# Held-back loads, block products for two more slabs, ScalarE copies and a new order at the end of a Fourier mixer with a gated FFN

## The chip, the core and the metric

The kernel runs on one core of a Trainium2 chip. A core has TensorE (matrix products, into PSUM banks), VectorE (DVE in the profile), ScalarE (ACT), GpSimd (POOL) and SyncE (SP, which issues most DMA transfers). Each engine works through its own instructions in order; semaphores tie the engines together. The metric is device microseconds of one execution, as the median of several runs; a profiled execution gives the trace.

## The reference, cut to what matters

```python
x = A_x                                   # 1 x 2048 x 640, bf16
xn = _layernorm(x, axis=-1)
s = irfft2(rfft2(xn, axes=(-2, -1)) * (w_r + 1j * w_i), s=(2048, 640))
g = silu((gelu(xn @ w_gate) * (xn @ w_up)) @ w_down)      # F = 1536
return x + s * g
```

So every row is normalized; the normalized matrix goes through a two-dimensional Fourier filter (s) and through a gated FFN (g), and the two meet in the last line. Layernorm is over the 640 columns, gelu is the tanh form, and everything is bf16 outside of the transform.

## The kernel before, in words

The 2048 rows are taken as 16 slabs of 128 rows (slab n1 holds the rows n1, n1+16, ...), `X[:, n1, :]`. Four slabs make a group g of 512 rows. For each group the FFN goes over 12 tiles of 128 hidden columns: a gate product (`psg`, five matmuls, then gelu by ScalarE into `ge`, L837), an up product (`psu`, five matmuls, L832), and on VectorE `psu * ge` into `UT` (L839). Then the down product: for groups 0 and 3 slab by slab (`down_third`, L967, 24 matmuls of 320 columns for a slab), for groups 1 and 2 as block products of two slabs (`product`, L933): seven products of six matmuls in place of 48 matmuls for a pair of slabs, over sums of blocks of `UT` that VectorE makes (`u_sum`, L907) and sums of blocks of Wd (`w_sum`). Results of products are copied out by ScalarE (L937) and added on VectorE (L947). Then silu (`gated`, L861 to L882) gives G.

`psg` and `psu` have two PSUM banks each, and so has the pool `psB`, which the transposes and all stages of the Fourier filter share.

The order of the work is written by hand. `back` is a list of 144 steps, most of them an FFN half tile (1.08 us of TensorE) or a product; `plan[s]` lists what is put behind step s, and `put` fills it. Instructions are issued in just that order, so it is also the order in every engine's queue. The Fourier filter is spread over the steps: forward stages (`slab_S1`, `slab_D`) during groups 0 and 1, a middle stage in eleven bursts (`s2_step`, from step `sb` = 67 on; its input comes through DRAM, ZDR to `B2`, and its result leaves through DRAM, UDR to V), inverse stages (`slab_S1i` L735, `slab_Di` L762, and the VectorE and ScalarE work of `group_cs`, `group_Y`, `group_rest` for three slabs at a time) during the products of group 2 and all of group 3. `finish(n1)` multiplies s by G (L811), adds x (for slabs 12 to 15 on VectorE, L815; for the others by an accumulating DMA) and writes out. It runs whenever a half of a slab is ready.

At the start SP loads x0, x1, then weights of Wu in twos of tiles between further slabs, and ScalarE's queue loads Wg (L231). The DMA semaphores are used in turn, eight of them, so the ninth transfer waits for the first one's landing, and so on. Statistics of a slab are two `bn_stats` halves and an aggregate on VectorE; the root of the variance comes from ScalarE for slab 0 (`root_act`) and from GpSimd for the others (`root`). `norm_parts` normalizes a slab in two parts, columns 0 to 384 and 384 to 640; `slab_Tparts` transposes those parts on TensorE and copies them to `xnT`. TensorE first runs 21 matmuls on constants (`warm_pe`, L588).

Of the kernel before, what the change touches and what calls it, by code (L numbers as in the profile page):

```python
# [10 lines left out]
BF16 = mybir.dt.bfloat16  # L11
# [3 lines left out]
P = 128  # L15
# [61 lines left out]
def build(nc, env):  # L77
# [19 lines left out]
    load_w(1, 2, 4)  # L97
    load_x(2, 1)
    load_w(1, 4, 6)
    load_x(3, 1)  # L100
    load_gu(6, 8)
    load_x(4, 4)
    load_gu(8, 12)
    load_x(8, 4)
    nc.sync.dma_start(out=Wd, in_=B_w_down.rearrange("(t p) d -> p t d", p=P))
    load_x(12, 4)

# [104 lines left out]
    def root_act(n1):  # L212
        rstd[n1] = c1("rst0")
        nc.scalar.activation(out=rstd[n1], in_=mva[n1 // 4][:, n1 % 4, 1:2], func=ACT.Abs_reciprocal_sqrt, bias=eps)
        nc.scalar.activation(out=warm, in_=negpi, func=ACT.Gelu_apprx_tanh)

# [110 lines left out]
    vt_iota(0)  # L327
    stats(0)
    bn_half(1, 0)
# [474 lines left out]
    def finish(n1):  # L804
        ks = [k for k in range(len(cut(n1)) - 1) if (n1, k) in left and (n1, k) in Gok]
        if ("y", n1) not in done or not ks:
            return
        sl = slice(cut(n1)[ks[0]], cut(n1)[ks[-1] + 1])
        G = Gt[n1 // 4]
        Y = st_c["Y"](n1, 1)[:, 0, sl]  # L810
        nc.vector.tensor_tensor(out=Y, in0=Y, in1=G[:, n1 % 4, sl], op=ALU.mult)  # L811
        if n1 < XA:
            nc.gpsimd.dma_start(out=Y, in_=xv[:, n1, sl], accum_op=ALU.add)  # L813
        else:
            nc.vector.tensor_tensor(out=Y, in0=Y, in1=xts[n1][:, sl], op=ALU.add)  # L815
        nc.sync.dma_start(out=outv[n1][:, sl], in_=Y)
        left.difference_update((n1, k) for k in ks)
# [3 lines left out]

    cur = {}

    ges = {}

    def ffn_piece(g, t, k, c0, c1_):
# [11 lines left out]
        else:  # L838
            nc.vector.tensor_tensor(out=UT[:, t, c0:c1_], in0=ps, in1=ges[t], op=ALU.mult)  # L839

    def ffn_part(g, t, h):
        for k in range(2):
            ffn_piece(g, t, k, h * 256, h * 256 + 256)

# [16 lines left out]
    def gated(g, j, k, ph, late=False):  # L861
# [19 lines left out]
        else:  # L881
# [4 lines left out]
    SS = {k: b[:, 0:2 * 6 * P].rearrange("p (i t c) -> p i t c", i=2, c=P)  # L886
          for k, b in (((1, 0), XG[:, 0, :]), ((1, 1), RX[:, 0, :]), ((2, 0), XG[:, 0, :]), ((2, 1), SB))}
    tf = Tfwd.rearrange("p n k -> p (n k)")
# [31 lines left out]
    def product(g, a, i):  # L920
# [50 lines left out]

    def ffn_slab(j, tk):
        for t, k in tk:
            ffn_piece(0, t, k, j * P, j * P + P)

    GG, UU = ((0, 0), (1, 0)), ((0, 1), (1, 1))

    def run(*items):
        for it in items:
            it[0](*it[1:])  # L980

    PARTS = ((0, 3), (3, 5))

# [15 lines left out]
    STR = (1, 2)  # L999
    back = [(run, (ffn_slab, 0, GG), (norm_parts, 1), (slab_Tparts, 1), (vt_iota, 1), (ffn_slab, 0, UU),  # L1000
             (inv_consts, 0), (inv_consts, 1)),
            (run, (ffn_slab, 1, GG + UU), (stats, 2), (root, 2, 1))]
    for h in range(2):
        for t in range(0 if h else 2, NP):
            back.append((ffn_part, 0, t, h))
        if h == 0:
            back[-1] = (run, (ffn_piece, 0, NP - 1, 0, 0, 256), (slab_Tparts, 3), (ffn_piece, 0, NP - 1, 1, 0, 256))
    for g in range(4):
# [14 lines left out]

    put(1, inv_rest)
    put(2, norm, 2)
    put(3, bn_half, 3, 0)
    put(4, bn_half, 3, 1)
    put(4, bn_join, 3)
    put(4, root, 3, 1)
    put(4, slab_T, 2, 1)  # L1030
    put(5, norm, 3)
    for g in range(5):
# [148 lines left out]
```

## Time and profile before

| what | value |
|---|---|
| median of 3 runs | 193.76 us (193.47 to 193.83) |
| the profiled execution | 193.65 us |
| its span, first to last instruction | 191.9 us, 4068 instructions |
| TensorE matmuls busy | 186.1 us (97%) |
| VectorE, ScalarE, GpSimd busy | 150.9, 131.9, 53.9 us |
| first FFN matmul starts | 6.84 us |
| last matmul starts its run / last VectorE instruction starts | 187.99 / 189.26 us |

How to read it: the span is shorter than the execution's own time by what lies before the first and after the last instruction. A busy TensorE is not TensorE at its peak, since its matmuls are pipelined and their ends are modelled: a matmul of 128 columns is shown with 219 ns while the next one starts 56 ns later. Line numbers (L832) are those of the kernel before.

### The profile page before, as it was taken

Reading aid. Unit: us, or ns where it says so; the run is one execution under the profiler, and the core shown is the slowest. Engines: PE = TensorE matmul, PEld = TensorE weight load, DVE = VectorE, ACT = ScalarE, POOL = GpSimd, SP = SyncE. Lnnn points to the kernel's source line nnn. Section 1 sums busy time; section 2 is a strip of 40 time slices with the busy share of each in tenths; the row PEclk is TensorE's granted clock in tenths of the full one; section 3 lists DMA queues with packets and bytes.
Section 4 is the critical chain, followed back from the end, with each engine's and each line's share of the span. In section 5 each row is a group of like instructions: output and inputs, shape, how many; then the busy total and the mean of one; then the engine's idle time right before and its main releaser. Section 6 shows DMA issues by size and latency. Waiting matters only on the chain.

```text
span 191.9 us, 4068 instructions
## 1 busy us (share of the span) xinstructions
PE 186.1 (97%) x1453; PEld 115.6 (60%) x1469; DVE 150.9 (79%) x364; ACT 131.9 (69%) x241; POOL 53.9 (28%) x91
## 2 busy tenths in 40 slices
PE   7999999999999999999999999999999999999993
PEld 5788854677655665566543334347775555556772
DVE  6787889899799889846978677685445898888973
ACT  4658557957878778536697878634989776876622
POOL 4458768999040200000000000002030134150400
PEclk9999999999999999999999999999999999999999
DMA  6999999948889994249996444149900084778842
GB/s 164 300 329 360 370 332 170 172 99 318 178 165 191 211 300 120 78 111 230 223 108 123 106 103 103 42 107 273 266 5 0 0 117 111 152 153 213 121 174 62
DMA packets 39700, 32.43 MB, mean 169 GB/s; under 512 B 12928, under 2 KB 37760, under 8 KB 39552
## 3 DMA queue, kind: packets, MB, share of 16 engines
q1 hardware_dynamic: 35888, 27.91, 58.6%
q0 software_dynamic: 1824, 3.28, 9.4%
q10 hardware_dynamic: 1968, 0.98, 1.9%
q8 instruction: 11, 0.18, 0.4%
q14 instruction: 9, 0.07, 0.1%
HBM read 19.03 MB, written 7.88 MB: 140 GB/s over the span
## 4 chain that ended last, share of the span: by engine, by line
PE 95%; DMA 2%; DVE 1%; issue 1%; SPq 0%; ACT 0%
PE psu L832 27%; PE psg L832 27%; PE psg L967 7%; PE psg L933 7%; PE psu L967 6%; PE psu L933 5%; PE pu L657 2%; PE pd L762 2%; PE pv L735 2%; PE pz L555 2%; PE pd L573 2%; PE px L628 2%; DMA X<-in_A_x_dram 2%; PE pt L994 1%; PE pd L575 1%
## 5 line engine op out<-in xcount | busy, mean ns | idle before, releaser
L832 PE MATMUL psu<-XG,Wu 128*128 128x512 bf16 (+2 forms) x284 | 60.4, 342 | 0.5 <-issue 0.3
L832 PE MATMUL psg<-XG,Wg 128*128 128x512 bf16 (+2 forms) x280 | 60.1, 341 | 0.6
L839 DVE TENSOR_TENSOR UT<-psu,ge 128x512 bf16<-128x512 f32 (+2 forms) x58 | 34.4, 594 | 13.6 <-PE psu L832 8.1
L837 ACT ACTIVATE ge<-psg 128x512 bf16<-128x512 f32 (+2 forms) x58 | 30.3, 523 | 21.3 <-PE psg L832 20.6
L832 PEld LDWEIGHTS <-Wu 128*128 128x128 bf16 x290 | 25.9, 98 | 20.9 <-issue 3.4
L832 PEld LDWEIGHTS <-Wg 128*128 128x128 bf16 x290 | 26.5, 98 | 18.8 <-issue 0.2
L967 PEld LDWEIGHTS <-UT 128*128 128x128 bf16 x204 | 19.1, 98 | 6.9
L813 POOL DMA_DIRECT2D VY<-in_A_x_dram x12 | 10.6, 964 | 26.2 <-ACT W L737 10.5
L713 POOL COPY vr<-VY 128x128 bf16<-128x128 bf16 x2 | 0.6, 291 | 60.2 <-DMA VY<-UDR 60.2
L644 DVE TENSOR_TENSOR RZ<-xs,W 128x960 bf16<-128x960 bf16 (+2 forms) x22 | 13.3, 647 | 4.4 <-ACT xs L640 4.4
L967 PE MATMUL psg<-Wd,UT 128*128 128x320 bf16 (+1 forms) x108 | 15.7, 290 | 0.0
L578 ACT CAST RZ<-pd 128x660 bf16<-128x660 f32 x16 | 11.3, 706 | 5.2 <-PE pd L575 5.2
L189 DVE BATCH_NORM_STATS2 st<-X 128x6 f32<-128x320 bf16 x32 | 14.0, 476 | 0.6 <-DMA X<-in_A_x_dram 0.4
L933 PEld LDWEIGHTS <-UT 128*128 128x128 bf16 x120 | 11.4, 98 | 4.8 <-issue 0.4
L967 PE MATMUL psu<-Wd,UT 128*128 128x320 bf16 (+1 forms) x96 | 13.9, 293 | 0.0
L737 ACT CAST W<-pv 128x640 bf16<-128x640 f32 x16 | 11.1, 691 | 3.1 <-PE pv L735 3.1
L763 ACT ACTIVATE W<-pd 128x640 bf16<-128x640 f32 x16 | 11.3, 706 | 1.5 <-PE pd L762 1.5
L557 ACT CAST GEN<-pz 128x640 bf16<-128x640 f32 x16 | 11.2, 698 | 1.2 <-PE pz L555 1.2
L672 ACT CAST RX<-pu 128x480 bf16<-128x480 f32 (+3 forms) x22 | 10.8, 489 | 1.1 <-DVE RX L672 0.3
L640 ACT CAST xs<-px 128x960 bf16<-128x960 f32 (+2 forms) x11 | 10.3, 933 | 0.0
L207 POOL TENSOR_TENSOR rst<-ve,mhalf 128x1 f32<-128x1 f32 (+1 forms) x6 | 5.5, 913 | 11.5 <-DVE ve L205 11.5
L933 PE MATMUL psg<-X,UT 128*128 128x320 bf16 x48 | 7.8, 300 | 0.0
(202 smaller groups left out, 302.1 us busy)
## 6 DMA issues: line engine op xcount, KB each, us to landing
ZDR<-RZ SPq DMA_DIRECT2D x16, 160.5 KB, 4.1
UDR<-RX SPq DMA_DIRECT2D x10, 240.8 KB, 3.1
B<-ZDR SPq DMA_DIRECT2D x8, 240.8 KB, 5.2
W<-UDR SPq DMA_DIRECT2D x2, 963.0 KB, 9.1
X<-in_A_x_dram SPq DMA_DIRECT2D x3, 640.0 KB, 10.3
Wd<-in_B_w_down_dram SPq DMA_DIRECT2D x1, 1920.0 KB, 14.6
VY<-in_A_x_dram POOLq DMA_DIRECT2D x12, 160.0 KB, 4.3
out_dram<-VY SPq DMA_DIRECT2D x12, 160.0 KB, 2.8
```

The source lines that it names most:

```text
L189: nc.vector.bn_stats(out=st_n[n1][:, k, :], in_=X[:, n1, 320 * k:320 * k + 320])
L557: nc.scalar.copy(out=Zt[n1], in_=pz)
L578: nc.scalar.copy(out=zd.rearrange("p c (q e) -> p c q e", e=10), in_=pd[:, :, 0:330].rearrange("p c (e q) -> p c q e", q=33))
L644: nc.vector.tensor_tensor(out=pp[-1], in0=xs, in1=WT[:, :, h0:h0 + n, l0:l0 + w], op=ALU.mult)
L672: copy(out=out, in_=src)
L737: nc.scalar.copy(out=vs, in_=pv)
L763: nc.scalar.activation(out=parts(eobuf, i, 5)[:, :, n1 - DG[i][0], :], in_=pd, func=ACT.Copy, scale=(2.0 if n1 // 4 in BY_SILU else 1.0) / ...
L832: nc.tensor.matmul(ps, lhsT=WT[:, c, t * P:(t + 1) * P], rhs=xnT[g][:, c, c0:c1_], start=(c == 0), stop=(c == 4))
L837: nc.scalar.activation(out=ges[t], in_=ps, func=ACT.Gelu_apprx_tanh)
L839: nc.vector.tensor_tensor(out=UT[:, t, c0:c1_], in0=ps, in1=ges[t], op=ALU.mult)
L933: nc.tensor.matmul(ps, lhsT=lhs[:, t, :], rhs=rhs[:, t, :], start=(t == 0 and i in (0, 1, 3)), stop=(t == 5), skip_group_check=i in (2, 4, ...
L967: nc.tensor.matmul(ph, lhsT=UT[:, t, j * P:(j + 1) * P], rhs=Wd[:, t, c0:c1_], start=(t == 0), stop=(t == NT - 1))
```

## The change

The change has five parts.

- The start. Wg and Wu of tiles 0 to 3 are loaded in two parts each, by rows (0 to 384, 384 to 640) and for four tiles at once. Wu's load is held back: GpSimd writes one element column of it from slab 0's first statistics, and the transfer waits for that write. Slab 2's load and all after it are held back in the same way by the first normalized part of slab 0. Slab 0 is normalized and transposed before the second half of slab 1's statistics; slab 1's root comes from ScalarE. Eighteen warm matmuls run before slab 0's transposes and four after them, in place of 21 and 2.
- Tiles 0 to 3 are done for one slab at a time with four tiles in one bank (`ffn_quad`), and tiles 4 to 7 (and 0 to 7 for slabs 2 and 3) for two slabs and two tiles in one bank (`ffn_multi`), so that gelu and the multiply take 512 columns at a time.
- The bursts of the middle stage start at step 65 in place of 67, and all that is placed after them moves with them.
- In group 3 the up products of tiles 6 to 11 are copied from PSUM to `UT` by ScalarE, and VectorE multiplies in place.
- Slabs 12 and 13 use block products (42 matmuls for 48), in an order interleaved with the thirds of slab 14; slab 15 follows. Slabs 12, 13 and 14 are finished only when both halves are there.

```diff
@@ load_w
-    def load_w(k, t0, t1, eng=nc.sync):
+    def load_w(k, t0, t1, eng=nc.sync, c0=0, c1_=5):
...
-        eng.dma_start(out=(Wg, Wu)[k][:, :, f0:f1], in_=(wgv, wuv)[k][:, :, f0:f1])
+        eng.dma_start(out=(Wg, Wu)[k][:, c0:c1_, f0:f1], in_=(wgv, wuv)[k][:, c0:c1_, f0:f1])
...
+    PARTS = ((0, 3), (3, 5))
...
     load_x(0, 1)
     load_x(1, 1)
-    load_w(1, 0, 2)
-    load_w(1, 2, 4)
-    load_x(2, 1)
-    load_w(1, 4, 6)
-    load_x(3, 1)
-    load_gu(6, 8)
...
@@ root_act
-        rstd[n1] = c1("rst0")
+        rstd[n1] = c1("rst%d" % n1)
...
+    def gelu_table():
...
-    for t in (0, 2, 4):
-        load_w(0, t, t + 2, nc.scalar)
+    for part in PARTS:
+        load_w(0, 0, 4, nc.scalar, *part)
...
-    stats(0)
+    bn_half(0, 0)
+    nc.gpsimd.tensor_copy(out=Wu[:, 0, 0:1], in_=st_n[0][:, 0, 0:1])
+    for part in PARTS:
+        load_w(1, 0, 4, nc.sync, *part)
+    bn_half(0, 1)
+    bn_join(0)
     bn_half(1, 0)
     root_act(0)
@@ finish
-        if ("y", n1) not in done or not ks:
+        if ("y", n1) not in done or not ks or (n1 in (12,13,14) and len(ks) < 2):
             return
...
+    UP_COPY = {3: range(6, 12)}
@@ ffn_piece
-            nc.vector.tensor_tensor(out=UT[:, t, c0:c1_], in0=ps, in1=ges[t], op=ALU.mult)
+            ut = UT[:, t, c0:c1_]
+            if t in UP_COPY.get(g, ()):
+                nc.scalar.copy(out=ut, in_=ps)
+                ps = ut
+            nc.vector.tensor_tensor(out=ut, in0=ps, in1=ges[t], op=ALU.mult)
+
+    def ffn_quad(k, j, *part):
...
+        ps = cur["m"].rearrange("p (t w) -> p t w", w=P)
+        WT = (Wg, Wu)[k]
+        for a, b in [PARTS[i] for i in part]:
+            for i in range(4):
+                for c in range(a, b):
+                    nc.tensor.matmul(ps[:, i, :], lhsT=WT[:, c, i * P:(i + 1) * P],
+                                     rhs=xnT[0][:, c, j * P:(j + 1) * P], start=(i + c == 0), stop=(c == 4),
+                                     skip_group_check=True)
+        if part[-1] == 1:
+            multi_out(k, 0, ps, j * P, j * P + P)
+
+    def ffn_multi(k, t0, n, c0, c1_, half=None):
...
+        for i in range(n) if half is None else range(half * n // 2, (half + 1) * n // 2):
+            for c in range(5):
+                nc.tensor.matmul(ps[:, i, :], lhsT=WT[:, c, (t0 + i) * P:(t0 + i + 1) * P], rhs=xnT[0][:, c, c0:c1_],
+                                 start=(c == 0), stop=(c == 4))
+        if half != 0:
+            multi_out(k, t0, ps, c0, c1_)
+
+    def multi_out(k, t0, ps, c0, c1_):
...
+        if k == 0:
...
+            nc.scalar.activation(out=ge, in_=ps, func=ACT.Gelu_apprx_tanh)
+        else:
+            nc.vector.tensor_tensor(out=UT[:, t0:t0 + n, c0:c1_], in0=ps, in1=ges[t0, c0], op=ALU.mult)
...
@@ product
-        if a == 0 and i in REST:
+        if a == 0 and i in REST and g in STR:
...
@@ slab_Tparts
-        for (a, b), ev in zip(PARTS, (nc.vector.tensor_copy, nc.scalar.copy)):
+        for (a, b), ev in zip(PARTS, (nc.vector.tensor_copy, nc.scalar.copy if n1 > 1 else nc.vector.tensor_copy)):
@@ back
+    back = [(run, (ffn_quad, 0, 0, 0, 1), (vt_iota, 1)),
+            (run, (ffn_quad, 1, 0, 0), (slab_Tparts, 1), (ffn_quad, 1, 0, 1)),
+            (ffn_quad, 0, 1, 0, 1),
+            (ffn_quad, 1, 1, 0, 1)]
+    for h, k, t0 in ((0, 0, 4), (0, 0, 6), (0, 1, 4), (0, 1, 6)) + tuple((1, k, t) for t in (0, 2, 4, 6) for k in range(2)):
+        back.append((ffn_multi, k, t0, 2, 256 * h, 256 * h + 256))
...
+        if g == 3:
+            items = [(product, 3, 0, i) if i < 7 else (down_third, 3) + divmod(i - 7 + 6, 3) for i in (0,7,2,1,4,8,3,9,6,5,10,11,12)]
+            back.append((run, *items[0:2]))
+            back.extend((run, it) for it in items[2:])
+            continue
...
+    put(128, u_sum, nc.vector, 3, 0, 0, TB)
+    put(131, u_sum, nc.vector, 3, 0, TB, 6)
...
-    sb = 67
+    sb = 65
...
-    warm_pe(21)
+    warm_pe(18)
+    norm_parts(0)
+    nc.gpsimd.tensor_copy(out=X[:, 2, 0:1], in_=X[:, 0, 0:1])
+    load_x(2, 1)
+    load_w(0, 4, 8)
+    load_x(3, 1)
+    load_w(1, 4, 8)
+    load_x(4, 4)
...
+    slab_Tparts(0)
+    warm_pe(4)
     bn_half(1, 1)
     bn_join(1)
-    root(1, 1)
-    norm_parts(0)
-    slab_Tparts(0)
-    warm_pe(2)
+    root_act(1)
+    gelu_table()
+    norm_parts(1)
```

More of the change, by code (lines that the diff above doesn't have):

```diff
@@ L838, in ffn_piece @@
         else:
[L839 to L843, printed above, removed]
+            ut = UT[:, t, c0:c1_]
[4 more added lines that the diff above has]
+    def ffn_quad(k, j, *part):
+        assert ("T", j) in done
+        if part[0] == 0:
+            cur["m"] = bank(k)
+        ps = cur["m"].rearrange("p (t w) -> p t w", w=P)
[9 more added lines that the diff above has]
+    def ffn_multi(k, t0, n, c0, c1_, half=None):
+        w = c1_ - c0
+        for j in range(c0 // P, c1_ // P):
+            assert ("T", j) in done
+        if half in (None, 0):
+            cur["m"] = bank(k)[:, 0:n * w].rearrange("p (t w) -> p t w", w=w)
+        ps = cur["m"]
+        WT = (Wg, Wu)[k]
+        for i in range(n) if half is None else range(half * n // 2, (half + 1) * n // 2):
[5 more added lines that the diff above has]
+    def multi_out(k, t0, ps, c0, c1_):
+        n, w = 512 // (c1_ - c0), c1_ - c0
+        flush()
+        if k == 0:
+            ge = work.tile([P, 512], BF16, tag="ge", bufs=3, name="ge")[:, 0:n * w].rearrange("p (t w) -> p t w", w=w)
+            ges[t0, c0] = ge
+            nc.scalar.activation(out=ge, in_=ps, func=ACT.Gelu_apprx_tanh)
+        else:
+            nc.vector.tensor_tensor(out=UT[:, t0:t0 + n, c0:c1_], in0=ps, in1=ges[t0, c0], op=ALU.mult)
     def ffn_half(g, t, k):
@@ L999, in build @@
     STR = (1, 2)
[L1000 to L1007, printed above, removed]
+    back = [(run, (ffn_quad, 0, 0, 0, 1), (vt_iota, 1)),
[4 more added lines that the diff above has]
+        back.append((ffn_multi, k, t0, 2, 256 * h, 256 * h + 256))
+    back[6] = (run, (ffn_multi, 1, 4, 2, 0, 256, 0), (slab_T, 2, 1), (ffn_multi, 1, 4, 2, 0, 256, 1))
+    back[7] = (run, (ffn_multi, 1, 6, 2, 0, 256, 0), (slab_Tparts, 3), (ffn_multi, 1, 6, 2, 0, 256, 1))
     for g in range(4):
@@ L1022, in put @@
         plan[s].append(item)
[L1024 to L1031, printed above, removed]
+    put(1, stats, 2)
+    put(1, root, 2, 1)
+    put(2, bn_half, 3, 0)
+    put(2, bn_half, 3, 1)
+    put(3, norm, 2)
+    put(3, bn_join, 3)
+    put(3, root, 3, 1)
+    put(3, inv_consts, 0)
+    put(3, inv_consts, 1)
+    put(4, inv_rest)
+    put(5, norm_parts, 3)
     for g in range(5):
@@ L1134, in build @@
             put(min(d + 8 + k, LAST), finish, n0 + k)
-    warm_pe(21)
+    warm_pe(18)
[6 more added lines that the diff above has]
+    load_x(4, 4)
+    load_gu(8, 12)
+    load_x(8, 4)
+    nc.sync.dma_start(out=Wd, in_=B_w_down.rearrange("(t p) d -> p t d", p=P))
+    load_x(12, 4)
+    slab_Tparts(0)
+    warm_pe(4)
     bn_half(1, 1)
     bn_join(1)
-    root(1, 1)
-    norm_parts(0)
-    slab_Tparts(0)
-    warm_pe(2)
+    root_act(1)
+    gelu_table()
+    norm_parts(1)
     put(5, phase_const)
```

12 lines of the change are left out of this document (1 added, 11 removed).

## The prediction

> **What bounds the kernel now.** I read the page's busy shares and its chain first, then the chain in order of time at both ends, then the timeline there.
>
> ```profile
> PE 186.1 (97%) x1453; PEld 115.6 (60%) x1469; DVE 150.9 (79%) x364; ACT 131.9 (69%) x241; POOL 53.9 (28%) x91
> PE 95%; DMA 2%; DVE 1%; issue 1%; SPq 0%; ACT 0%
> ```
>
> TensorE holds 95% of the chain. From matmul start to matmul start I find hardly a stall between 6.05 and 188 us that is not a missing record. So VectorE and ScalarE time in the middle is worth nothing by itself; the two ends and TensorE's own work are worth something.
>
> ```profile
> 1.17 3.19 DMA X<-in_A_x_dram
> 4.38 0.90 DVE st L189 x2
> 5.70 0.30 DVE X L218
> 6.05 0.54 PE pt L994 x5
> 6.84 0.76 PE psg L832 x10
> ...
> 187.99 0.68 PE psg L967 x12
> 188.69 0.28 ACT XG L867
> ```
>
> At the start the chain goes through the statistics of slab 1 (4.38), although the first matmuls need slab 0 alone:
>
> ```profile
> 1.18 4.55 PE L588 MATMUL psg<-GEN 128*128 128x256 bf16 x21 [1.18 <-DVE eps L229]
> 4.29 0.29 ACT L214 ACTIVATE rst<-mva,eps 128x1 f32<-128x1 f32 x1 [2.08 <-DVE mva L195]
> 4.60 1.28 ACT L215 ACT_TABLE_LOAD   x1
> 5.62 0.63 DVE L218 TENSOR_SCALAR X<-X,mva,rst 128x384 bf16<-128x384 bf16 x2
> ```
>
> Slab 0's root is there at 4.58, but its normalization starts at 5.62, since VectorE does slab 1's second half, its aggregate and an add first. That second is what the reordering can win.
>
> **Part 1, the start.** x0 and x1 land as before (3.10 and 4.36 by the trace's landing events), for both go first on SP's queue in both kernels. After slab 1's first half (4.38 to 4.83) the normalization of slab 0 starts at 4.83 in place of 5.62. The transposes follow 0.43 later (5.62 to 6.05 before), so at 5.26; the two copies out are both VectorE's now, 0.36 and about 0.3, done at 6.35 with the first at 6.11; the four warm matmuls fill the wait. The first Wg matmul starts at 6.16, not 6.84: -0.68. Then 80 matmuls of 128 columns at 56 ns and 5 transposes (0.28) reach 10.9 or so; the old kernel had the same columns done at 11.58, so the lead stays about 0.6 if nothing is late. I keep -0.6.
>
> What could be late: slab 1's transposes need its norm, which now stands behind copies, second half (0.48), aggregate (0.21) and a root on ScalarE (0.29): norm at 7.4, transposes at 7.8; TensorE is at 8.0 there. The table load for gelu (1.28) now follows both roots, so the first gelu ends at 9.25, while its bank is wanted again at 11. Both covered, by 0.2 and 1.7.
>
> The loads carry the real risk. Wu waits on SP for a POOL copy that waits for slab 0's first statistics (3.6) and stands behind an iota that ends at 3.75: issue at about 4.1. Behind it in SP's queue stand all later loads; slab 2's waits a second time, for a POOL copy after the norm (about 5.4). Landing of Wu's first part (384 KB): the 160 KB of x0 took 2.4 us from issue, 224 KB more at the 342 GB/s of the window from 4 to 5 us add 0.7: 7.2. By the 1.8 us of the 160 KB output writes it is 6.6, by the 6.1 us median of the old 320 KB weight loads (behind others in their queue) 10.2. TensorE wants it at 7.35. I take 7.0, since x0, x1 and Wg (960 KB) are nearly through by 5.4 and nothing else is in the way. Tiles 4 to 7 of Wg come to 10.0 (1,200 KB from 5.4 at some 330 GB/s, estimate), wanted at 11. The later weights need two fewer issues and have 1 KB rows where they had 512 B; they come no later than before.
>
> **Part 2, the bursts two steps earlier** (65 for 67, with all that hangs on them). The transfers that burst 0 reads landed at 86.55 and 87.63; TensorE would be there at 88.04 in the same reckoning: 0.4 of cover. But now three bursts, not two, fall among the products of group 1, where VectorE is full:
>
> ```profile
> 89.67 0.32 PE px L628 x2
> 92.55 0.32 PE px L628 x2
> 92.87 0.42 PE pu L657 x5
> ```
> ```profile
> 91.41 1.24 DVE L644 TENSOR_TENSOR RZ<-xs,W 128x960 bf16<-128x960 bf16 x2 [1.52 <-ACT xs L640]
> ```
>
> Laying VectorE's queue out with these durations, the products of burst 1 end about 93.85 and TensorE asks at 93.5 to 93.7: a stall of 0.2. Bounds -0.1 (a late burst at 103.26 or 118.28 shows 0.3 of stall each today, and one burst fewer is there) and +0.6. In the products of group 2 the inverse slabs start two steps earlier, which loads ScalarE (4.00 of 4.00 us busy from 136 to 140) by two casts (0.69 and 0.71), but they fall into its idle time at 130 to 133. I cost this at 0; without that cover it is up to 0.5.
>
> **Part 3, up products copied by ScalarE** (six tiles of group 3):
>
> ```profile
> L839 DVE TENSOR_TENSOR UT<-psu,ge 128x512 bf16<-128x512 f32 x40 | 27.5, 687 | 11.7 <-PE psu L832 6.9 <-ACT ge L837 3.4 <-ACT RX L672 0.9
> L491 DVE TENSOR_TENSOR Y<-Y,X 128x512 bf16<-128x512 bf16 x4 | 1.7, 424 | 0.1
> ```
>
> VectorE saves 6 x (687 - 424) = 1.6 us; ScalarE pays 6 x 0.59 (between its 320-column copy, 0.43, and its 640-column cast, 0.70). The trace shows the two rates of the multiply. The Trainium skill ("VectorE: DVE Perf Modes", Rules for kernel authors) advises the copy out of PSUM only for several operations on it, and here there is one; by that rule the product of the last tile is merely 0.33 later, which the slack in part 4 holds, so the sum would be the same. TensorE is the bound there, so the relief is worth 0 by itself; it pays for the sums below.
>
> **Part 4, block products for slabs 12 and 13.** 48 matmuls of 320 columns become 42: 6 x 0.136 (1.63 per 12) = -0.82. Added on VectorE: the sums for group 3 (3 x 0.48, 3 x 0.22, 0.58) and three adds (0.49 each), 4.1 us; on ScalarE three copies (0.43). Call T the end of the last up matmul. The last tile: ScalarE's copy T+0.1 to 0.7; VectorE is in inverse work until T+0.9, multiplies (0.42) to 1.3, and makes the two sums that product 2 reads (0.22 each) by T+1.8. TensorE does product 0 (0.82) and a third of slab 14 (1.09) meanwhile, and reads the last sum at T+2.6. Next on VectorE stand a third sum, slab 8 to 11's last finish and six inverse instructions (2.6 us, starts 0.08 closer than durations as in the timeline), then the add of product 1, done at T+4.9; product 3 wants its bank at 5.4. Then 0.58 of sums, 1.16 and three short inverse instructions, and the next add, done at T+7.7, wanted by product 5 at 8.2. So VectorE is busy from T on with 0.4 us in hand. I charge no stall; 0.5 if it runs late.
>
> **Part 5, the last slabs whole.** One output write fewer, but the order at the end changes:
>
> ```profile
> 187.50 0.33 DVE L811 TENSOR_TENSOR X<-X,XG 128x320 bf16<-128x320 bf16 x1 [0.42 <-ACT XG L867]
> 187.86 0.32 DVE L815 TENSOR_TENSOR X<-X,RX 128x320 bf16<-128x320 bf16 x1
> 188.39 0.26 DVE L811 TENSOR_TENSOR X<-X,XG 128x192 bf16<-128x192 bf16 x1 [0.20 <-ACT XG L867]
> 188.68 0.26 DVE L815 TENSOR_TENSOR X<-X,RX 128x192 bf16<-128x192 bf16 x1
> 189.00 0.23 DVE L811 TENSOR_TENSOR X<-X,XG 128x128 bf16<-128x128 bf16 x1
> 189.26 0.23 DVE L815 TENSOR_TENSOR X<-X,RX 128x128 bf16<-128x128 bf16 x1
> ```
>
> Today VectorE ends 0.84 after the last matmul (188.65), with 0.2 idle inside. Slab 12, whose last half comes from product 5, is now finished between the 187.86 and the 188.39 instruction of this list: two of 640 columns, 0.4 and 0.53 start to start. With the idle time used up, VectorE ends about 1.45 after the last matmul: +0.6 (from +0.3 to +0.8). What follows, the last write and the end (2.4 us), stays.
>
> **Sum.** -0.6 + 0.2 - 0.82 + 0.6 = -0.6. The profiled execution took 193.65 (span 191.87 and 1.78 around it), the median is 193.76, so 193.05 and 193.15: I say **193.1**.
>
> **Rivals.** *Late loads (slower).* If Wu's first part lands after 7.35, TensorE waits one for one; at 0.6 of lateness the gain is gone, from 8.4 on the kernel is slower, and with 6.1 us to landing (10.2) it takes 193.1 + 2.85 = 196.0. For it: no load of the old start landed in less than 2.4 us. Against: the queue ahead is short. 0.17. *The ends eat it (no change).* VectorE's chain in the tail runs 0.4 us behind my layout, or the third burst stalls 0.6: 193.5 to 193.9. For it: 7.24 of 8 us busy from 176 to 184 today, with more put in. 0.18. *More is won.* No burst stall, and the tail of VectorE only 0.3 longer: 193.1 - 0.2 - 0.3 = 192.6 or less. 0.12. *The clock comes later (slower).* The 21 warm matmuls run at 213 ns each until 5.4, the transposes at 6.05 at 57 ns; with 18 of them TensorE rests from 5.02 to 5.26. Should the full clock come one such stretch of some 4 us later, 128-column matmuls at 107 ns for 3.4 us cost 1.7: 194.8. The Trainium skill ("TensorE: Matmul & The Clock Gate", Part 1) has a window of about 3.4 us that runs freely and must be busy; the trace's 4.2 us of slow matmuls agree with it. A rest of 0.24 is small against it: 0.05.
>
> **Chances.** The forecast, with its own range 192.6 to 193.4, has 0.48. A measurement of this kernel tells about 0.2% (0.39 us) from no change. Faster: 0.48 and 0.12; same: 0.18; slower: 0.17 and 0.05. The range goes down to 192.3 and up to 194.5, which leaves out the worst of the late loads and of the clock.
>
> **What would show it.** First Wg matmul at 6.1 to 6.3 and no wait for Wu or Wg; the first up matmul of the second half near 16.0; a gap of 0.2 before the second output matmuls of the bursts; products that end without gaps; VectorE's last instruction 1.3 to 1.6 after the last matmul. A TensorE gap around 7.3 or 11 would make it wrong.

## The result, and the profile after

The changed kernel takes 194.96 us (median; 194.36 to 195.71 but for one at 197.35) against 193.47 for the kernel before: a ratio of 1.0067, with a 95% interval of 1.0057 to 1.0077. It is 1.5 us slower by the medians and 1.3 by the ratio; the forecast was 0.6 faster, and the time lies above the upper end of the range. The profiled execution is the one at 197.35: in it alone the granted clock fell to half for 3.4 us behind the wait shown below, which is worth 1.7 us, so its times after 13.6 are to be read less that amount.

The busy shares, the clock by slices and the chain of the page after:

```profile
PE 187.2 (96%) x1466; PEld 116.7 (60%) x1482; DVE 152.1 (78%) x364; ACT 133.9 (68%) x239; POOL 53.2 (27%) x92
...
PEclk9987999999999999999999999999999999999998
...
PE 90%; DMA 5%; DVE 2%; issue 1%; ACT 0%; SPq 0%; POOL 0%
```

TensorE had 95% of the chain and now has 90%; DMA went from 2% to 5%. The chain in order of time (start, duration, what) names the transfer:

```profile
4.62 0.39 DVE X L211
5.01 0.05 issue
5.07 0.24 POOL X L1180
5.31 0.02 issue
5.33 0.34 SPq L84
5.67 0.04 issue
5.71 7.73 DMA Wg<-in_B_w_gate_dram
13.44 0.05 issue
13.48 4.02 PE psg L869 x20
```

Here is the second hold, step by step: the normalized part of slab 0 (4.62), GpSimd's one-column copy (5.07), the issue of slab 2 on SP (5.33), and behind it the issue of tiles 4 to 7 of Wg at 5.71. They land at 13.44. TensorE's timeline beside it:

```profile
6.42 1.45 PE L853 MATMUL psg<-XG,Wg 128*128 128x128 bf16 x20
7.72 0.83 PE L853 MATMUL psu<-XG,Wu 128*128 128x128 bf16 x12
...
10.28 1.28 PE L853 MATMUL psu<-XG,Wu 128*128 128x128 bf16 x20
13.48 4.02 PE L869 MATMUL psg<-XG,Wg 128*128 128x256 bf16 x20 [1.93 <-DMA Wg<-in_B_w_gate_dram]
```

The last 128-column matmul starts at 11.34; then TensorE stands still for 2.1 us. The x20 after it takes 4.02 us where the same 20 matmuls took 2.35 in *no_holds*, a run below: this is the clock at half. Stretch by stretch (length, then busy times of PE, PEld, DVE, ACT and POOL, then the granted clock, the DMA share and GB/s):

```profile
12.00:13.00 1.00, 0.00 (x0) 0.00 (x0) 0.00 (x0) 0.00 (x0) 0.00 (x0) 1.00 1.09 413
...
14.00:15.00 1.00, 1.00 (x7) 0.71 (x5) 1.00 (x3) 0.00 (x0) 0.00 (x0) 0.50 1.03 369
...
17.00:18.00 1.00, 1.00 (x12) 0.89 (x10) 0.41 (x3) 0.45 (x1) 0.82 (x3) 1.00 1.13 380
```

At the other end, VectorE and TensorE:

```profile
190.19 0.33 DVE L809 TENSOR_TENSOR X<-X,XG 128x320 bf16<-128x320 bf16 x1 [0.32 <-ACT XG L906]
190.54 0.33 DVE L813 TENSOR_TENSOR X<-X,RX 128x320 bf16<-128x320 bf16 x1
190.79 0.48 DVE L809 TENSOR_TENSOR X<-X,XG 128x640 bf16<-128x640 bf16 x1
191.31 0.49 DVE L813 TENSOR_TENSOR X<-X,RX 128x640 bf16<-128x640 bf16 x1
...
192.43 0.23 DVE L813 TENSOR_TENSOR X<-X,RX 128x128 bf16<-128x128 bf16 x1
```
```profile
190.50 0.83 PE L1006 MATMUL psg<-Wd,UT 128*128 128x128 bf16 x12
```

VectorE ends at 192.66, 1.33 us after the last matmul (191.33). Slab 12's two instructions of 640 columns stand where the prediction put them.

I cut both traces at the same instructions (starts from the timeline), to see where the time went:

| stretch | before | after |
|---|---|---|
| first Wg matmul starts at | 6.84 | 6.42 |
| from there to the end of tile 11 of group 1 | 75.33 | 79.33 |
| from there to the last matmul's start (products of group 1 to slab 15) | 106.27 | 105.37 |
| last matmul's end to VectorE's end | 0.84 | 1.33 |
| VectorE's end to the end of the span | 2.38 | 2.91 |

Behind the start TensorE gained 0.90; 0.49 of it was given back up to VectorE's end and 0.53 more behind that. The rest was lost in the start: 4.0 us from the first Wg matmul on in this execution, of which 2.1 are the wait and 1.7 the clock. Without the clock's 1.7 this execution would still be 0.7 above the median, so the wait of a typical execution may be shorter than 2.1; only this one has a trace.

The 0.53 is a term that the prediction took as fixed ("the last write and the end (2.4 us), stays"). The last write landed 1.59 after VectorE's end, in place of 1.47, and the program ended 1.32 after that landing, in place of 0.91: SP has four semaphore waits of some 0.06 left there in place of one, and VectorE's closing DRAIN starts at 195.23, 0.3 behind those of the other engines. With the old start and parts 2 to 5 the stretch is 2.56 (*old_start*), with the new start without holds 2.58 to 3.00 in eight kernels. Why it differs stays open.

### The profile page after: what moved, and what is told of

It is laid out like the page before. It is cut to its first block, busy times and chain, and to the rows that moved or that the text cites. A ratio compares the mean times of both kernels' runs of the same rounds, so it can differ in the third digit from the quotient of the medians.

```text
span 195.6 us, 4072 instructions
## 1 busy us (share of the span) xinstructions
PE 187.2 (96%) x1466; PEld 116.7 (60%) x1482; DVE 152.1 (78%) x364; ACT 133.9 (68%) x239; POOL 53.2 (27%) x92
## 4 chain that ended last, share of the span: by engine, by line
PE 90%; DMA 5%; DVE 2%; issue 1%; ACT 0%; SPq 0%; POOL 0%
PE psu L831 22%; PE psg L831 22%; PE psg L972 9%; PE psu L972 6%; PE psg L1006 5%; PE psg L869 4%; PE psu L1006 4%; DMA Wg<-in_B_w_gate_dram 4%; PE psu L869 3%; PE pu L655 2%; PE pv L733 2%; PE pd L760 2%; PE pz L553 2%; PE pd L571 2%; PE px L626 2%; DMA X<-in_A_x_dram 1%
## 5 line engine op out<-in xcount | busy, mean ns | idle before, releaser
L831 PE MATMUL psu<-XG,Wu 128*128 128x512 bf16 x194 | 49.0, 379 | 0.5 <-issue 0.3
L831 PE MATMUL psg<-XG,Wg 128*128 128x512 bf16 x190 | 48.7, 379 | 0.5
L836 ACT ACTIVATE ge<-psg 128x512 bf16<-128x512 f32 x40 | 23.9, 597 | 14.3 <-PE psg L831 13.5
L842 DVE TENSOR_TENSOR UT<-psu,ge 128x512 bf16<-128x512 f32 x34 | 23.4, 687 | 9.9 <-PE psu L831 5.2
L831 PEld LDWEIGHTS <-Wu 128*128 128x128 bf16 x200 | 18.0, 98 | 20.2 <-issue 3.2
L831 PEld LDWEIGHTS <-Wg 128*128 128x128 bf16 x200 | 18.6, 98 | 18.0
L972 PEld LDWEIGHTS <-UT 128*128 128x128 bf16 x150 | 14.2, 98 | 6.1 <-issue 0.6
L1006 PEld LDWEIGHTS <-UT 128*128 128x128 bf16 x156 | 14.5, 98 | 4.9
L1006 PE MATMUL psg<-Wd,UT 128*128 128x320 bf16 (+1 forms) x84 | 12.1, 288 | 0.0
L880 ACT ACTIVATE ge<-psg 128x512 bf16<-128x512 f32 x8 | 4.8, 595 | 9.9 <-PE psg L869 8.6
L869 PE MATMUL psg<-XG,Wg 128*128 128x256 bf16 x60 | 9.0, 312 | 1.9 <-DMA Wg<-in_B_w_gate_dram 1.9
L1006 PE MATMUL psu<-Wd,UT 128*128 128x320 bf16 (+1 forms) x72 | 10.4, 290 | 0.0
## 6 DMA issues: line engine op xcount, KB each, us to landing
Wd<-in_B_w_down_dram SPq DMA_DIRECT2D x1, 1920.0 KB, 14.2
```

The source lines that it names most:

```text
L831: nc.tensor.matmul(ps, lhsT=WT[:, c, t * P:(t + 1) * P], rhs=xnT[g][:, c, c0:c1_], start=(c == 0), stop=(c == 4))
L836: nc.scalar.activation(out=ges[t], in_=ps, func=ACT.Gelu_apprx_tanh)
L842: nc.vector.tensor_tensor(out=ut, in0=ps, in1=ges[t], op=ALU.mult)
L869: nc.tensor.matmul(ps[:, i, :], lhsT=WT[:, c, (t0 + i) * P:(t0 + i + 1) * P], rhs=xnT[0][:, c, c0:c1_], start=(c == 0), stop=(c == 4))
L972: nc.tensor.matmul(ps, lhsT=lhs[:, t, :], rhs=rhs[:, t, :], start=(t == 0 and i in (0, 1, 3)), stop=(t == 5), skip_group_check=i in (2, 4, ...
L1006: nc.tensor.matmul(ph, lhsT=UT[:, t, j * P:(j + 1) * P], rhs=Wd[:, t, c0:c1_], start=(t == 0), stop=(t == NT - 1))
```

## The experiments

Theory at the outset: the loads of the start come late ("late loads"). Rival: the tail or the bursts cost more than was charged ("the ends eat it"). Parts are numbered as in the prediction: part 1 is the start with its new order of tiles 0 to 7 (the first two points of the list of the change), part 2 the bursts, part 3 the copies by ScalarE, part 4 the block products, part 5 the last slabs whole.

### The change cut in two

*old_start* is the kernel before with parts 2 to 5, *start_alone* the kernel after without them.

```diff
@@ old_start, on the kernel before
+ UP_COPY, product(3, 0, i), sums for group 3, slabs 12 to 14 whole
-    sb = 67
+    sb = 65
```
```diff
@@ start_alone, on the kernel after
- UP_COPY, product(3, 0, i), sums for group 3, slabs 12 to 14 whole
-    sb = 65
+    sb = 67
```

> The kernel before with parts 2 to 5 of the change (bursts two steps earlier, ScalarE copies, block products for slabs 12 and 13, last slabs whole) and the old start. Theory 'late loads' (the wait of TensorE for tiles 4 to 7 of Wg, 11.4 to 13.48 in the trace of the changed kernel, is what was missed): parts 2 to 5 sum to 0.0 as predicted, so this takes 193.2 to 193.8 beside 193.47 for the kernel before. Rival 'the ends eat it' (the tail or the bursts cost more than charged): 194.5 to 195.0, for then the start is not to blame.

> The changed kernel with parts 2 to 5 undone, so that only the start differs from the kernel before. 'Late loads': -0.6 as predicted for the start and +1.4 to 2.1 for the wait, so 194.3 to 195.0. 'The ends eat it': 192.9. The wait before the first matmul with tiles 4 to 7 of Wg is there in the trace by the first theory, 1.5 us or more.

Measured: *old_start* 193.32, ratio 0.9983 (0.9974 to 0.9993); *start_alone* 195.10 (median of five), ratio 1.0089 (1.0058 to 1.0121). A sixth execution of the latter, the profiled one, took 1,106.52 us for a reason that nothing here shows, so no trace tells whether the wait for tiles 4 to 7 is there. Parts 2 to 5 win 0.33 us, a little more than the 0.0 predicted, and the start costs 1.7 (1.1 to 2.3) where -0.6 was predicted. "The ends eat it" falls.

### The loads: hold, width, order

Six edits of the kernel after, each about the loads alone.

```diff
@@ no_hold2
-    nc.gpsimd.tensor_copy(out=X[:, 2, 0:1], in_=X[:, 0, 0:1])
@@ no_hold1
-    nc.gpsimd.tensor_copy(out=Wu[:, 0, 0:1], in_=st_n[0][:, 0, 0:1])
@@ no_holds
- both lines
@@ twos (and no_holds_twos: the same with both lines taken away)
-    load_w(0, 4, 8)
+    load_w(0, 4, 6)
+    load_w(0, 6, 8)
...
-    load_w(1, 4, 8)
+    load_w(1, 4, 6)
+    load_w(1, 6, 8)
@@ one_queue, on no_holds
     load_x(1, 1)
+    for part in PARTS:
+        load_w(0, 0, 4, nc.sync, *part)
...
-    for part in PARTS:
-        load_w(0, 0, 4, nc.scalar, *part)
```

> The changed kernel without the second hold alone: slab 2's transfer and all behind it follow Wu's two parts in SP's queue without waiting for the first normalized part of slab 0. Theory 'issued late': tiles 4 to 7 of Wg were issued at 5.71 because of the hold, and from 7.5 to 9.5 the DMA engines had too little queued (204 to 233 GB/s in half microseconds there, 340 to 377 just before); now issued about 1 us earlier, these tiles land at 12.4 or earlier for 13.44, and the time falls by 1.0 or more, to 194.0 or less. Rival 'one wide transfer': four tiles are waited for as one transfer, and its slowest DMA engine is 3.4 us behind its fastest; taking the hold away changes that little: 194.6 to 195.0.

> The changed kernel with tiles 4 to 7 of Wg and of Wu in two transfers of two tiles each in place of one of four; holds as they are. Theory 'one wide transfer': tiles 4 and 5 land about half a transfer earlier, at 11.5 to 12, the wait of 2.1 us shrinks to 0.5 or less and tiles 6 and 7 cost at most 0.5 more, so 193.3 to 194.0. Theory 'issued late': the first pair lands at 12.5 or later, since the engines are starved before 9.5 either way, and little is won: 194.4 or more.

> The changed kernel without either hold: Wu's two parts and all later loads follow x0 and x1 in SP's queue at once; Wg's two parts stay on ScalarE's queue, transfers of four tiles. Theory 'issued late': SP's queue never runs dry, 2,400 KB at 345 GB/s from 2.0 us put tiles 4 to 7 of Wg at 9.0 on the mean DMA engine and at 10.2 to 11.4 on the slowest, so the wait of 2.1 us is gone or 0.3 at most: 192.6 to 193.3. Rival 'one wide transfer' as the whole cause: its slowest engine stays 2.4 to 3.4 us behind, the tiles land after 12 and 194.0 or more remains. What speaks against the whole idea: Wu's parts now share the engines with Wg's first parts, whose landing may slip from 5.19 to 6.3, with a wait of up to 0.4 before the first Wg matmul or within it.

> Without either hold, and tiles 4 to 7 of Wg and Wu in twos. With two tiles the DMA engines were 1.1 us apart at the landing (10.37 to 11.45) in place of 2.4 to 3.4 for four, so here both theories give no wait at these tiles: 192.4 to 193.0, the same as without the holds alone if the queue's running dry was the whole cause, 1 us or more below it if the wide transfer was.

> The changed kernel with all loads of the start in one queue in the order of need, x0, x1, Wg's two parts, Wu's two parts and then the rest, and without either hold. Without the holds the wait moved from tiles 4 to 7 of Wg to Wg's own second part (0.49 and 0.90 us), which shared the DMA engines with Wu. If that sharing was the cause, one queue in order serves it first, at 345 GB/s by about 5.6, and no wait for a load is left: 0.3 to 0.6 below the run without holds, so 193.2 to 193.5. If TensorE then only waits later, for VectorE's copy of slab 3's transposes (0.15 to 0.32 at 16.7 in the run without holds), the gain is 0.2 or less.

> The changed kernel without the first hold alone: Wu's two parts follow x0 and x1 at once, slab 2 and all behind it still wait for the first normalized part of slab 0. If the first hold parts the DMA engines, tiles 4 to 7 of Wg land before 11.4 as without both holds, and the time is 193.6 to 194.0. If any hold does it, because a transfer that is served as it is issued gets 130 to 280 GB/s and one with others queued ahead of it 350, these tiles land at 11.5 to 13 and 194.2 to 195.0 is measured.

Measured. The waits are those of TensorE's rows; the landing is that of tiles 4 to 7 of Wg (first and last of the 16 DMA engines, by the trace's landing events; for the kernels with twos, tiles 4 and 5, then 6 and 7):

| kernel | first Wg matmul | waits for loads | tiles land | ratio (95%) |
|---|---|---|---|---|
| after | 6.42 | 1.93 tiles 4 to 7 | 10.08 to 13.44 | 1.0067 (1.0057, 1.0077) |
| no_hold2 | 5.77 | 0.46 Wu, 0.94 tiles 4 to 7 | 9.88 to 12.24 | 1.0081 (1.0061, 1.0102) |
| no_hold1 | 5.83 | 1.49 Wg, second part | 9.42 to 11.59 | 1.0064 (1.0038, 1.0089) |
| twos | 5.86 | 1.09 Wu, first part | 9.27 to 10.36, 10.37 to 11.45 | 1.0049 (1.0032, 1.0066) |
| no_holds | 5.99 | 0.49 Wg, second part | 9.53 to 10.24 | 1.0003 (0.9985, 1.0020) |
| no_holds_twos | 5.96 | 0.90 Wg, second part | 8.84 to 9.71, 9.93 to 10.80 | 1.0009 (0.9994, 1.0024) |
| one_queue | 6.30 | 0.20 Wu, first part | 9.65 to 11.08 | 1.0027 (1.0013, 1.0042) |

Three things follow. First, both holds together cost 0.64%, 1.2 of the 1.3 us that the ratio shows: without them the kernel is level with the one before. Taking one of them away wins nothing: without the second, tiles 4 to 7 land 1.2 us earlier and are still late; without the first they land before TensorE asks for them (12.29), but only since TensorE is 1.49 late by then, for Wg's second part, which shares the DMA engines with Wu and lands at 8.11 in place of 5.84. So *no_hold2* went against "issued late" as the whole cause, which expected 194.0 or less, and *twos* against "one wide transfer", which expected 193.3 to 194.0. Second, the width shows in the landings, but hardly in the time. In *twos* the tiles were in time, and a wait for Wu came in their place; its interval overlaps that of the change. Without holds, four tiles at once landed with their engines 0.7 apart (9.53 to 10.24), and twos won nothing more. Third, the wait always moves to another load, so that the times expected of *no_holds* (193.3 at most), *no_holds_twos* (193.0) and *one_queue* (193.5) were all missed. The stretches show what the holds do to the rate; first the kernel after, then *no_holds*:

```profile
5.00:6.00 1.00, 1.00 (x9) 0.80 (x9) 0.66 (x4) 0.00 (x0) 0.23 (x1) 1.00 0.82 183
...
7.50:9.50 2.00, 2.00 (x39) 1.99 (x37) 0.98 (x6) 1.62 (x3) 1.56 (x4) 1.00 0.89 235
9.50:11.50 2.00, 2.00 (x37) 1.88 (x34) 1.73 (x5) 0.98 (x2) 0.11 (x1) 1.00 1.04 342
```
```profile
5.00:6.00 1.00, 1.00 (x11) 0.84 (x11) 0.66 (x3) 0.00 (x0) 0.00 (x0) 1.00 1.10 366
...
7.50:9.50 2.00, 2.00 (x39) 1.99 (x37) 0.91 (x6) 1.60 (x3) 1.56 (x4) 1.00 1.10 351
9.50:11.50 2.00, 2.00 (x39) 2.00 (x37) 1.93 (x6) 0.97 (x2) 0.06 (x1) 1.00 1.11 358
```

Twice, once behind each hold, the rate drops, to 183 and 235 GB/s in place of 366 and 351. The engines were idle in part (the DMA share is 0.82 and 0.89, not 1.10), but they were slower too: by the rows above each KB took 73 and 62 ns of engine time in place of 49 and 51. The median packet of 1 KB took 46 ns; what differs are long ones. Of the packets of 1 and 1.25 KB that began in the two windows, 16 of 179 and 28 of 437 took over 100 ns (up to 853), against 6 of 357 and none of 666 in *no_holds*. An empty queue is not the whole cause: by 7.5 SP had issued four more transfers behind slab 2 (5.71 to 7.23). And the engines fell apart: slab 2 landed within 1.6 us on the 16 engines and the tiles behind it within 3.4. The Trainium skill ("DMA: Bandwidth & Descriptors", section "Why a DMA increments its semaphore by 16 and not by 1") says that a transfer runs on up to 16 engines that finish independently and that only the full count means that all has landed; the trace agrees, for TensorE started 0.04 after the last engine (13.44) and not at 10.08. The long packets may be one cause, but the trace does not say on which engine a packet ran, and what makes them long stays open. Neither is bound to holds: from 4 to 12 us *one_queue* has 29 long packets and the engines 1.4 apart at tiles 4 to 7, and *burst67* (below), with the old start, has 3 and the engines up to 2.4 apart.

The new wait in *no_holds*, and one more, not for a load:

```profile
5.99 0.83 PE L852 MATMUL psg<-XG,Wg 128*128 128x128 bf16 x12
7.31 0.62 PE L852 MATMUL psg<-XG,Wg 128*128 128x128 bf16 x8 [0.49 <-DMA Wg<-in_B_w_gate_dram]
...
16.68 1.25 PE L868 MATMUL psg<-XG,Wg 128*128 128x256 bf16 x10 [0.15 <-DVE XG L1026]
```

TensorE's lead of 0.85 at the first Wg matmul was gone by 25.4: 0.65 at 7.31 and 0.32 at 16.68, start to start. The second is VectorE's copy of slab 3's transposes, behind a multiply of 0.69.

### Is the earlier start worth 0.6 once no load is late?

Four kernels without holds, with slab 12 finished sooner (below), and other orders of the first loads. In *two_deep*, SP's queue has x0 and the first parts of Wg and Wu, ScalarE's x1 and the second parts. *two_deep_swap* gives the first copy of slab 3 to ScalarE. *x_first* has the swap too and takes x1 back to SP, behind x0; *paired* exchanges the parts of its two queues.

```diff
@@ two_deep: SP's queue, then ScalarE's
     load_x(0, 1)
-    load_x(1, 1)
+    for k in range(2):
+        load_w(k, 0, 4, nc.sync, *PARTS[0])
...
-    for part in PARTS:
-        load_w(0, 0, 4, nc.scalar, *part)
+    load_x(1, 1, nc.scalar)
+    for k in range(2):
+        load_w(k, 0, 4, nc.scalar, *PARTS[1])
@@ two_deep_swap, slab_Tparts
-  (nc.vector.tensor_copy, nc.scalar.copy if n1 > 1 else nc.vector.tensor_copy)
+  (nc.scalar.copy, nc.vector.tensor_copy) if n1 > 1 else (nc.vector.tensor_copy, nc.vector.tensor_copy)
@@ x_first, paired
     load_x(0, 1)
+    load_x(1, 1)
...
-    load_x(1, 1, nc.scalar)
```

> The changed kernel without holds, x0 and the first parts of Wg and Wu on SP's queue, x1 and the second parts on ScalarE's, and slab 12 finished ahead of slab 15's first half. Both queues are filled ahead and in the order of need, so at 350 GB/s Wg is there by 6.0 and Wu's first part by 6.6: no wait for a load. If part 1's gain exists, the time is 0.6 below the old start with slab 12 finished sooner, 192.5 to 192.8. If TensorE then waits for VectorE's copy of slab 3 instead, 0.32 and the 0.5 that the loads no longer take, the gain is 0.0 to 0.2: 193.0 to 193.4.

> The same, and of slab 3's transposes the first part (384 columns) is copied out by ScalarE and the second by VectorE, the other way round than in the change. If VectorE's copy behind a multiply of 0.69 was what TensorE waited for at 16.7, 0.3 to 0.6 us are won over the run before it; if ScalarE is as late as VectorE there (it is in a constant's sine of 0.5 until about then), nothing.

> As the last (two filled queues, slab 12 finished sooner, ScalarE copying the first part of slab 3), but x1 on SP's queue right behind x0, then the first parts of Wg and Wu; the second parts alone on ScalarE's queue. If the reordered start is worth what the prediction said once no load is late, slab 1 lands at 4.1, the first Wg matmul starts at 5.9, no wait follows, no run shows the longer time, and it takes 0.5 to 0.8 less than the old start with slab 12 finished sooner: 192.3 to 192.7. If Wu's first part, now third in its queue, lands after 7.0, or a copy or a norm on VectorE holds TensorE by 16.5, half of it or all is gone: 192.8 to 193.3. Should a third of the runs be 1.6 us longer again, the rest before the transposes is not what made them so.

> As the run before it, with the parts exchanged: x0, x1 and the second parts of Wg and Wu on SP's queue, the first parts on ScalarE's, where Wg's first part starts as early as in the change. It should land at 5.3 to 5.6 and the second by 6.2, Wu's first by 7.0. If the reordered start is worth 0.6 once no load is late, 192.3 to 192.7; if a wait for Wg or Wu appears again (over 0.3 us in all), the gain goes to it: 192.9 to 193.5, and then no order of these loads that was tried lets the earlier start be used.

Measured: *two_deep* 1.0017 (0.9991 to 1.0044), *two_deep_swap* 1.0017 (0.9992 to 1.0043), *x_first* 0.9990 (0.9973 to 1.0006), *paired* 0.9995 (0.9982 to 1.0007). None reaches the 0.6 us: all lie above the old start with slab 12 finished sooner (0.9975, below), by which they are to be judged. TensorE's starts in *two_deep* and *two_deep_swap*:

```profile
5.94 0.72 PE L1027 MATMUL pt<-ident,X 128*128 128x128 bf16 x5 [0.74 <-DVE X L212]
...
7.30 2.34 PE L852 MATMUL psg<-XG,Wg 128*128 128x128 bf16 x20
```
```profile
5.86 0.54 PE L1027 MATMUL pt<-ident,X 128*128 128x128 bf16 x5 [0.76 <-DVE X L212]
...
6.68 1.28 PE L852 MATMUL psg<-XG,Wg 128*128 128x128 bf16 x20
...
16.52 1.25 PE L868 MATMUL psg<-XG,Wg 128*128 128x256 bf16 x10
```

No wait for a load, as expected; but x1 landed at 5.1 and 5.0, VectorE takes its statistics ahead of slab 0's norm, and the lead is gone before it begins. The swap took the wait for slab 3's copy from 0.32 (at 18.48 in *two_deep*) to 0.08 (at 16.52). *x_first* and *paired*:

```profile
7.56 1.29 PE L852 MATMUL psg<-XG,Wg 128*128 128x128 bf16 x20 [1.43 <-DVE X L213]
```
```profile
7.03 0.62 PE L852 MATMUL psg<-XG,Wg 128*128 128x128 bf16 x8 [0.22 <-DMA Wg<-in_B_w_gate_dram]
8.05 0.84 PE L852 MATMUL psu<-XG,Wu 128*128 128x128 bf16 x12 [0.40 <-DMA Wu<-in_B_w_up_dram]
```

The first row names VectorE, whose norm was long done (5.35); what landed just before is a weight part, at 7.51. In *paired* the first matmul is early (5.98), and the two waits and some short stalls take 1.1 us by 25.5. So in every order tried the lead went to a load, to slab 1 or to slab 3's copy. That 0.6 could be had with all of them in time was not shown, and is not excluded.

*two_deep* and *two_deep_swap* each show two groups of executions, two thirds at 193.2 to 193.9 and a third at 194.9 to 195.6, 1.7 and 1.6 us apart. Both profiles have the same rest (0.74, 0.76) before the transposes. The one of the longer group has 20 matmuls in 2.34 us and runs at half pace until 9.65, the other has them in 1.28. The clock records of the traces fit this: the stretches at full clock are whole multiples of 3.413 us in every profile read (187.73, 55 of them, in twelve of seventeen), so the clock is set at marks 3.41 us apart, which lie elsewhere in each execution. In *two_deep_swap* full clock begins at 4.87, ahead of the rest; in *two_deep* the mark at 6.26 came just behind it, and full clock began at the next, 9.67. So where the rest lies between the marks seems to decide; two profiles do not prove it, but no other kernel with twelve executions shows the two groups, and *x_first*, without that rest, does not. Ahead of the first record the granted clock of the views reads 1.00: there the spacing of the matmuls tells (107 ns, then 56), not that column.

### The terms behind the start

```diff
@@ burst67, on old_start
-    sb = 65
+    sb = 67
@@ no_copies, on old_start
-    UP_COPY = {3: range(6, 12)}
+    UP_COPY = {}
@@ slab12_sooner, on old_start, down_third
             if t == NT - 1:
+                if g == 3 and j == 3:
+                    flush()
                 gated(g, j, k, ph)
```

*one_queue_slab12* is *one_queue* with the last edit.

> The old start with parts 3 to 5, but the bursts at step 67 as before. Part 2 of the prediction charged 0.2 us to the earlier bursts: then this is 0.2 faster, 193.1. The trace of the old start with parts 2 to 5 has them in another way: 0.20 us more from the first products of group 1 to the last up tile, and 0.28 less after it, since inverse work left the tail: then this is 0.1 slower in TensorE's work, and slower still by what VectorE gets more to do in the tail, 193.4 to 194.0.

> The old start with parts 2, 4 and 5, but the up products not copied out by ScalarE. Part 3 of the prediction says that the 1.6 us it takes off VectorE are worth nothing by themselves but pay for the sums and adds of part 4, which had 0.4 us in hand: then this costs 0.5 to 1.2 us, 193.8 to 194.5. If VectorE has more in hand than that, it takes the same as with the copies, 193.2 to 193.4.

> The old start with parts 2 to 5, and slab 12 finished ahead of slab 15's first half on VectorE. In the trace of the old start with parts 2 to 5 VectorE ends 1.32 us after the last matmul and rests 0.32 just ahead of slab 15's first half (186.50). If VectorE's chain sets the end, as part 5 of the prediction has it, this rest is filled and the kernel ends 0.3 earlier: ratio to the kernel before about 0.9967, for 0.9983. If the output writes set the end, nothing changes.

> The same start, and slab 12 finished ahead of slab 15's first half. The latter took 0.15 us off the old start's version in the median (193.32 to 193.14) and filled the rest of 0.32 on VectorE; so 0.15 to 0.3 below the one queue alone. With both, 192.7 to 193.2 is expected, 0.2 to 0.4% under the kernel before.

Measured: *burst67* 195.90, ratio 1.0115 (1.0090 to 1.0140); *no_copies* 0.9993 (0.9980 to 1.0006); *slab12_sooner* 193.14, 0.9975 (0.9962 to 0.9988); *one_queue_slab12* 1.0015 (0.9999 to 1.0030), beside 1.0027 without the edit.

*burst67* is the surprise: parts 3 to 5 without the two steps of part 2 are 2.2 us slower than the kernel before. Its TensorE near the end:

```profile
183.02 0.98 PE L938 MATMUL psu<-X,XG 128*128 128x320 bf16 x6 [0.66 <-DVE Tfwd L952]
...
186.43 0.98 PE L938 MATMUL psu<-Wd,UT 128*128 128x320 bf16 x6 [0.53 <-DVE Y L952]
```

Both products wait for an add that stands behind two steps more of inverse work on VectorE. From group 1's products to the last matmul it takes 106.98 us, against 105.37 in *old_start*, and 0.35 more lie behind the last matmul: 2.0 of the 2.6 between the medians. The two profiled executions are 3.4 apart; the other 1.4 of that is in the start, where this one waited 0.22 for Wu and 0.78 for tiles 4 and 5 of Wg: the old start too has loads that are at times late.

*no_copies*: no product waits in its trace, and the 0.5 to 1.2 us more that part 3 of the prediction would ask for did not come; the 1.6 us that ScalarE takes off VectorE are worth 0.1%, which the intervals do not tell from nothing. *slab12_sooner* fills VectorE's rest as expected:

```profile
186.19 0.48 DVE L811 TENSOR_TENSOR X<-X,XG 128x640 bf16<-128x640 bf16 x1
186.71 0.49 DVE L815 TENSOR_TENSOR X<-X,RX 128x640 bf16<-128x640 bf16 x1
187.12 0.32 DVE L811 TENSOR_TENSOR X<-X,XG 128x320 bf16<-128x320 bf16 x1
...
188.43 0.22 DVE L815 TENSOR_TENSOR X<-X,RX 128x128 bf16<-128x128 bf16 x1
```

VectorE ends at 188.65, where *old_start* had 188.97. In time that is 0.08% in one pair and 0.12% in the other, of the right sign and inside the intervals. The old start with parts 2 to 5 and this order is the fastest kernel of the study, 0.25% under the kernel before. *one_queue_slab12* missed the 0.2 to 0.4% under the kernel before that were expected of it.

## Why the prediction was wrong, point by point

- **Part 1, the landing of Wg's tiles 4 to 7: the step that failed.** "1,200 KB from 5.4 at some 330 GB/s" was put at 10.0 (by those figures it is 9.1) for a want at 11; it was 13.44 for a want at 11.4. The estimate ran the engines at their full rate from the moment of the hold, where the rate was 183 and 235 GB/s in the windows above, and it asked when the mean engine is done, where the slowest one counts, 3.4 us behind the first. The runs without holds show that 1.2 of the 1.3 us by the ratio come and go with the holds. So the overlap of the held loads with TensorE's first 80 matmuls, which the sum took as free (-0.6 in all), is what failed.
- **Part 1, VectorE's order: right, and worth nothing so far.** The first Wg matmul came at 5.77 to 5.99 in the kernels with this order and x1 and Wg's first part in time (6.16 predicted; 6.42 in the profile after and 6.30 in *one_queue*, where the four warm matmuls ran at 213 ns). The lead was then spent on waits: for Wu's first part (7.0 predicted; 7.58 in the change, 7.4 and 8.1 in *no_hold2* and *twos*), Wg's second, or slab 3's copy at 16.5, which the prediction had not priced.
- **Part 2: wrong in sign, and in what it is for.** +0.2 was predicted, as a wait for VectorE at burst 1. No such wait came: the product behind that burst starts 0.10 late, as in the kernel before. From group 1's products to the last up tile the change did take 0.19 us more, but that this is the predicted size is chance: TensorE runs 80 inverse matmuls (L760) there in place of 75, 0.28 us that have left the stretch behind the last up tile, and the gaps around the bursts are 0.09 less. That makes -0.09 in all. And without it part 4 stalls TensorE by 1.5 us, start to start, in *burst67*: the two steps are what pays for the sums, and not the copies. One reading was false: the 0.32 after a late burst at 103.26 (and at 118.28, with the same count) is no stall. The kernel before, then *old_start*, behind a burst:

```profile
102.52 0.58 PE L657 MATMUL pu<-RZ,N 64*64 64x483 bf16 x8
103.26 1.03 PE L832 MATMUL psu<-XG,Wu 128*128 128x512 bf16 x4 [0.16 <-issue]
```
```profile
103.18 0.58 PE L657 MATMUL pu<-RZ,N 64*64 64x480 bf16 x8
103.69 1.25 PE L833 MATMUL psu<-XG,Wu 128*128 128x512 bf16 x5
```

  A tile has five matmuls of 512 columns and the first kernel's row counts four: a missing record of 0.22 of the 0.32. In *old_start*, with all five recorded, 0.10 is left, as at every other burst.
- **Part 3: right.** Worth nothing measurable, as said; that "it pays for the sums below" was not, since VectorE kept up without it. The Trainium skill ("VectorE: DVE Perf Modes", Rules for kernel authors) would copy out of PSUM only for several operations, and no run here contradicts it.
- **Part 4: right.** No product stalls in the changed kernel; -0.90 on TensorE for parts 2 and 4 together, of which -0.82 were predicted for part 4. That VectorE keeps up hangs on part 2, which the prediction did not say.
- **Part 5: right in kind.** +0.49 measured up to VectorE's end, +0.6 predicted. What follows did not stay at 2.4: it was 2.91 in the change and 2.56 in *old_start*. Parts 2 to 5 sum to -0.4 in the trace up to VectorE's end and to -0.33 by the ratio; 0.0 was predicted.
- **The rivals.** "Late loads" happened, with another load than the one it named, at the gap around 11 that the last paragraph of the prediction gave as the sign. "The clock comes later" was priced at 1.7, and two kernels of the study show 1.6 and 1.7; in the change itself it decides nothing but the one execution at 197.35. "The ends eat it" did not happen.

## What to carry to other kernels

A transfer that is held back until the right moment is not only issued later: here those behind the two holds ran at a half and two thirds of the rate that they had without holds, and the slowest engine set the landing. Price a hold by the latest landing of what stands behind it, not by the bytes over the full rate. When two parts of a change share an engine, ask which of them gives the other its slack before charging it as a cost, and count a tile's matmul records before calling a gap a stall.

## What was not expected of the hardware

- The 16 engines of one queue, 0.4 to 1.3 us apart at the landings of the kernel before until 14.2, were 3.4 us apart from the first transfer of four tiles behind both holds, and stayed so over the five transfers after it (20.93 for the last against 17.56 for the first). Without holds, the same transfer had them 0.55 to 1.42 apart in seven kernels. These are single profiles, and *burst67* had up to 2.4 with the old start and no hold.
- In the one profile of the change, a rest of TensorE of 2.1 us was followed by 3.4 us at half the granted clock (13.58 to 17.00). Rests of 1.49 us (*no_hold1*) and 1.43 (*x_first*) were not: the matmuls behind them were 56 ns apart. *x_first* has one execution of 196.42 with a mean granted clock of 0.991, where the profiled one has 1.00; it may be the same. The Trainium skill ("TensorE: Matmul & The Clock Gate", Part 1) gives an idle window of about 3.4 us as what brings the clock down; in this trace it came down behind a rest of 2.1, which fills 63% of the 3.41 us between two marks (10.17 and 13.58). The 1.43 of *x_first* fill 42%, and the 1.49 of *no_hold1* lie on both sides of a mark (7.58). Where between the two shares the clock comes down was not measured.
